# Attention scores and post-mixing on 64x128 tiles of the matmul array, v's products on 128x64 tiles, a group's query rows spaced out

## The chip, the core and the metric

The kernel runs on one core of a Trainium2 chip. The metric is the device time of one execution in microseconds (us). A core has a matmul engine (TensorE, PE in the rows; PEld is its weight load), VectorE (DVE), ScalarE (ACT), GpSimd (POOL) and SyncE (SP), and 16 DMA engines that the queues of SP, ACT and POOL share.

## What is computed

Attention whose heads are mixed before and after the softmax ("talking heads"), then a two-layer network with a PReLU. Batch 4, 12 heads, 448 positions, head width 64; all in float32, the network's weights in float64.

```python
scores = scale * np.matmul(q, k.transpose(0, 1, 3, 2))
scores = np.einsum('bhij,hg->bgij', scores, w_pre)
attn = softmax(scores)                       # over j
attn = np.einsum('bhij,hg->bgij', attn, w_post)
x = np.matmul(attn, v)                       # heads side by side: 1792 x 768
h = x @ w_in                                 # 768 x 2048
out = (np.maximum(h, 0) + alpha * np.minimum(h, 0)) @ w_out
```

## The kernel before

The first stage, up to some 523 us, is the attention; a second, from 555 us, is the network (lines 394 to 494), which the change does not touch. Between them lies the tail of the attention and the first loads of the network.

The attention works on chunks of query rows, four per batch (`CHUNKS`, line 27: 110, 110, 110 and 118 rows), 16 in all, and inside a chunk on groups of 10 rows, 180 in all, two of them per step, 90 steps. What happens to a group:

- `qk` (line 139): for a pair of heads, one in the upper 64 rows of the array and one in the lower, the chunk's scores for all 448 keys. A matmul here has at most 64 stationary columns, so a chunk's rows are cut in two (64 and 46, or 64 and 54), and the four pieces stand in the four 64x64 quarters of the array. `qk_out` (150) copies them from PSUM to the tile `st`, where a query row is a partition that holds all 12 heads. Six such pairs make a chunk.
- `relay` (159): a DMA from SBUF to SBUF takes the 10 rows of a group, partitions r to r+9 of `st` with 12 heads each, to 120 partitions of one of eight `sr` buffers. 180 relays of 210 KB are issued alternately by SP and POOL, three steps ahead of their use (`relays`, 338; a relay waits until the mix four steps back has read its buffer).
- `mix` (164): the mixing before the softmax, 64x64 tiles, two groups of a step side by side, four matmuls. `rmax`, `exp`, `norm` (173 to 194): row maximum on VectorE, two exponentials with their sums on ScalarE, and the scaling of the post-mixing weights `r`.
- `post` (196): two steps later the mixing after the softmax, with `e` as the stationary operand, 64 keys (columns) at a time, and 60 columns of `r` streamed: 28 matmuls per step. Its result is the one PSUM tile `pa`, keys in partitions; `post_out` (207) copies it into `at` with two ScalarE copies.
- `pv` (216): when a chunk is complete, for six heads at a time, v's product: 42 matmuls, in which `v` is the stationary operand (64 keys by 64 columns of one head) and `at` is streamed. Even and odd 64-key blocks are summed in two PSUM banks apart, and `pv_out` (230) copies one with ScalarE and adds the other with VectorE. The result goes to DRAM.

Each float32 matmul of the program is two weight loads and two matmul instructions in the trace. `qk` and `pv` use one PSUM tile in turns (`ps_s`, one buffer). The order is written by hand in `step` (349): the mix of the next step, the relays, VectorE's and ScalarE's part of the softmax, the first scores or v job of the step, `post` and `post_out`, further jobs. Beside this, VectorE rounds the network's weights from float64 (`round_f64`, seven instructions for each of 32 pieces), which POOL loads (`cr`) and SP stores (`wsc`).

Of the kernel before, what the change touches and what calls it, by code (L numbers as in the profile page):

```python
# [22 lines left out]
GI = 10  # L23
# [3 lines left out]
CHUNKS = [(0, 110), (110, 110), (220, 110), (330, 118)]  # L27
CW = 118
# [3 lines left out]
NS = 4  # L32
NJ = S // 64
# [27 lines left out]
def talking_heads_prelu(ctx: ExitStack, tc: tile.TileContext, q, k, v, w_pre, w_post, mask, w_in, w_out, alpha, out):  # L61
# [60 lines left out]
    def load_q(ci, dmas=None):  # L122
        b, c = chunk_list[ci]
        c0, cn = CHUNKS[c]
        q_t[ci] = qp.tile([128, NP, CW], F32, tag="q", name=f"q{ci}")
        for hf in range(2):
            dma = dmas[hf] if dmas else nc.gpsimd
            dma.dma_start(out=q_t[ci][64 * hf:64 * hf + 64, :, :cn],
                          in_=q[b, :, H * c0 + NP * hf * cn:H * c0 + NP * (hf + 1) * cn])

    def load_v(b):
        v_t[b] = vp.tile([128, NS, DM], F32, tag="v", name=f"v{b}")
        nf = S // 128
        nc.gpsimd.dma_start(out=v_t[b][:, :nf, :], in_=v[b, :nf * 128].rearrange("(s p) n -> p s n", p=128))
        nc.gpsimd.dma_start(out=v_t[b][:S - nf * 128, nf, :], in_=v[b, nf * 128:])
# [3 lines left out]
    def qk(ci, p, ps_pool=None):  # L139
        b, c = chunk_list[ci]  # L140
        cn = CHUNKS[c][1]
        ps = (ps_pool or ps_s).tile([128, 2, 512], F32, tag="m" if ps_pool else "s", name=f"s{ci}_{p}")
        for lo in range(0, cn, 64):
            hi = min(lo + 64, cn)
            for hf in range(2):
                r = slice(64 * hf, 64 * hf + 64)
                nc.tensor.matmul(ps[lo:hi, hf, :S], q_t[ci][r, p, lo:hi], k_t[b][r, p, :], start=True, stop=True)  # L147
        u_t["qk", ci, p] = ps
# [10 lines left out]
    def relay(n, dma):  # L159
        ci, r = groups[n]  # L160
        sr_t[n] = sr_b[n % NSR]
        dma.dma_start(out=sr_t[n][SR0:SR0 + GP], in_=s_t[ci][r:r + GI])  # L162
# [33 lines left out]
    def post(m):  # L196
        e, r = e_t.pop(m), r_t.pop(m)
        for u in range(2):
            for jb in range(NJ):
                s, c = divmod(jb, 2)  # L200
                for g in range(2):
                    h = slice(64 * g, 64 * g + 64)
                    dst = pa[64 * c:64 * c + 64, g, s * GP:(s + 1) * GP].rearrange("p (h i) -> p h i", h=H)
                    nc.tensor.matmul(dst[:, :, HI * u:HI * u + HI], e[h, u, 64 * jb:64 * jb + 64],  # L204
                                     r[h, u].rearrange("p (h i) -> p h i", h=H), start=True, stop=True)

    def post_out(m):
        for g in range(2):
            n = 2 * m + g
            ci, r = groups[n]  # L210
            if n == first[ci]:
                a_t[ci] = ap_.tile([128, NS, H, CW], F32, tag="a", name=f"at{ci}")
            dst = a_t[ci].rearrange("p s h i -> p (s h) i")[:, :, r:r + GI]
            nc.scalar.copy(dst, pa[:, g, :NS * GP].rearrange("p (s i) -> p s i", i=GI))  # L214

    def pv(ci, hx, ps_pool=None):
# [71 lines left out]
    with tc.manual_schedule():  # L288
# [23 lines left out]
        nc.vector.memset(pa, 0.0)  # L312
# [218 lines left out]
```

## Time and profile before

| | us |
|---|---|
| Three runs | 1031.63, 1038.42, 1039.06; median 1038.42 |
| Profiled execution, first to last instruction | 1038.9 |
| first stage, from the first mix to the last | 27 to 523: 496 |
| between the stages | 523 to 555: 32 |
| second stage | 555 to 1039: 484 |

The profiled execution's span lies 0.5 us above the median, and the parts are read as parts of that span. Over the whole span PE is busy 84%, PEld 66%, DVE 48%, ACT 43% and POOL 34%.

How to read the rows: "busy" is the time in which at least one instruction of the kind ran. "Idle <-X" is time in which an engine did nothing, and X what ended it; "issue" means that it waited for nothing that the profile shows. PEclk is the granted share of TensorE's full clock. The DMA share is the mean busy share of the 16 DMA engines. An x84 behind a form counts instructions, and sizes are partitions x elements; "64*64" is the piece of the array that a matmul uses, rows by columns.

### The profile page before, as it was taken

What the parts mean: (1) busy time and instruction counts of PE and PEld (TensorE: products, weight loads), DVE (VectorE), ACT (ScalarE), POOL (GpSimd) and SP (SyncE); (2) the same over time, 40 slices, a digit from 0 to 9 for tenths busy, and PEclk for the clock granted to TensorE, in tenths of its full rate; (3) what the DMA queues carried; (4) which work ended last, traced back from release to release, by engine and by line L of the source; (5) the groups of instructions that cost most, each with busy time, mean ns of one, the idle gap of its engine ahead of it and who ended that gap; (6) DMA issues with size and microseconds to landing.
All of it is one profiled execution on the core that took longest, in us unless ns stands there. A gap on an engine that the chain in (4) does not pass through costs nothing.

```text
span 1038.9 us, 26286 instructions
## 1 busy us (share of the span) xinstructions
PE 869.1 (84%) x11540; PEld 687.8 (66%) x11540; DVE 500.2 (48%) x886; ACT 441.6 (43%) x870; POOL 348.7 (34%) x305
## 2 busy tenths in 40 slices
PE   4656767867868687778666999999999999999998
PEld 2134444544535355455455999999999999999997
DVE  3454666656657376758624224632265224542222
ACT  1453666655657466648342232323233323232322
POOL 3121222222212122211004455554455454545452
PEclk9687898988889798889796999999999999999999
DMA  7698878897899977898618600020001000010001
GB/s 149 154 185 193 173 190 204 220 220 179 167 228 213 200 191 181 186 247 176 145 32 316 271 1 19 1 89 1 1 19 63 27 1 9 9 54 1 1 1 53
DMA packets 55209, 123.86 MB, mean 119 GB/s; under 512 B 21080, under 2 KB 38840, under 8 KB 54712
## 3 DMA queue, kind: packets, MB, share of 16 engines
q0 software_dynamic: 15232, 59.01, 25.7%
q1 hardware_dynamic: 38546, 60.12, 20.7%
q10 hardware_dynamic: 1318, 3.08, 1.2%
q8 instruction: 90, 1.47, 0.6%
q14 instruction: 23, 0.19, 0.1%
HBM read 59.85 MB, written 23.59 MB: 80 GB/s over the span
## 4 chain that ended last, share of the span: by engine, by line
PE 67%; DMA 16%; ACT 7%; issue 5%; DVE 4%; SPq 1%; POOL 0%; ACTq 0%; DVEq 0%; POOLq 0%
PE h L435 23%; PE acc L460 23%; DMA sr<-st 14%; PE s L147 7%; PE x L226 6%; PE m L170 4%; PE pa L204 4%; ACT st L155 3%; ACT at L214 2%; ACT e L182 1%; DMA xr<-x 1%; DMA wb<-in_w_post_dram 1%; DMA cr<-in_w_out_dram 1%; DVE xe L236 1%; DVE nm L175 1%
## 5 line engine op out<-in xcount | busy, mean ns | idle before, releaser
L435 PE MATMUL h<-xs,wi 128*128 128x448 f32 x1152 | 251.4, 371 | 12.6 <-DVE xs L425 11.3
L460 PE MATMUL acc<-g,wo 128*128 128x448 f32 x1152 | 248.2, 368 | 0.0
L435 PEld LDWEIGHTS h<-xs,wi 128*128 128x128 f32 x1152 | 218.4, 190 | 35.4 <-issue 11.5
L460 PEld LDWEIGHTS acc<-g,wo 128*128 128x128 f32 x1152 | 216.2, 188 | 21.8
L413 POOL TENSOR_TENSOR wi<-wr,wi 128x768 fp32r<-128x768 f32 x64 | 118.6, 1853 | 269.8 <-ACT wi L412 269.8
L204 PEld LDWEIGHTS pa<-r,e 64*64 64x64 f32 x5040 | 115.4, 146 | 79.6 <-issue 55.4
L175 DVE TENSOR_REDUCE nm<-m 128x2 f32<-128x896 f32 x90 | 97.9, 1088 | 135.7 <-PE m L170 135.5
L444 DVE TENSOR_SCALAR t<-h,alpha_sb 128x448 f32<-128x448 f32 x64 | 43.8, 684 | 245.7 <-PE h L435 245.7
L204 PE MATMUL pa<-r,e 64*64 64x60 f32 x5040 | 121.9, 234 | 43.6 <-issue 33.8
L170 PE MATMUL m<-sr,wk 64*64 64x448 f32 (+1 forms) x720 | 111.6, 650 | 50.4 <-DMA sr<-st 43.2
L446 ACT CAST g<-t 128x448 fp32r<-128x448 f32 x64 | 36.3, 567 | 275.2 <-DVE t L445 275.2
L162 POOL DMA_DIRECT2D sr<-st x88 | 54.2, 617 | 276.9 <-PE m L170 185.0
L147 PE MATMUL s<-k,q 64*46 64x448 f32 (+2 forms) x768 | 112.7, 640 | 39.5 <-ACT st L155 27.8
L214 ACT COPY at<-pa 128x480 f32<-128x480 f32 x180 | 93.2, 572 | 82.2 <-PE pa L204 82.0
L413 POOL TENSOR_TENSOR wo<-wr,wo 128x768 fp32r<-128x768 f32 x64 | 123.8, 1935 | 7.6 <-ACT wo L412 5.9
L182 ACT ACTIVATE e<-m,nm 128x448 f32<-128x448 f32 x180 | 113.7, 646 | 14.2 <-DVE nm L175 14.2
L226 PEld LDWEIGHTS x<-at,v 64*64 64x64 f32 x2688 | 88.2, 146 | 37.6 <-issue 20.3
L155 ACT COPY st<-s 110x896 f32<-110x896 f32 (+1 forms) x93 | 84.6, 909 | 63.0 <-PE s L147 55.6
L226 PE MATMUL x<-at,v 64*64 64x110 f32 (+1 forms) x2688 | 92.6, 280 | 18.5 <-issue 13.3
L147 PEld LDWEIGHTS s<-k,q 64*64 64x64 f32 (+2 forms) x768 | 27.5, 140 | 92.3 <-ACT st L155 70.9
L170 PEld LDWEIGHTS m<-sr,wk 64*64 64x64 f32 (+1 forms) x720 | 29.3, 151 | 77.5 <-issue 64.7
L412 ACT CAST wo<-wr 128x768 fp32r<-128x768 f32 x64 | 53.8, 841 | 62.3 <-PE acc L460 62.3
(46 smaller groups left out, 564.1 us busy)
## 6 DMA issues: line engine op xcount, KB each, us to landing
sr<-st SPq DMA_DIRECT2D x89, 210.0 KB
sr<-st POOLq DMA_DIRECT2D x88, 210.0 KB, 9.7
cr<-in_w_in_dram POOLq DMA_DIRECT2D x16, 768.0 KB, 11.5
cr<-in_w_out_dram POOLq DMA_DIRECT2D x16, 768.0 KB, 10.1
wsc<-ct SPq DMA_DIRECT2D x32, 384.0 KB
wr<-wsc SPq DMA_DIRECT2D x14, 768.0 KB
xr<-x SPq DMA_DIRECT2D x24, 224.0 KB
out_dram<-o SPq DMA_DIRECT2D x24, 224.0 KB
```

Of the source, the lines that this page charges most:

```text
L147: nc.tensor.matmul(ps[lo:hi, hf, :S], q_t[ci][r, p, lo:hi], k_t[b][r, p, :], start=True, stop=True)
L155: copy(dst[:cn, p], u_t.pop(("qk", ci, p))[:cn, :, :S])
L162: dma.dma_start(out=sr_t[n][SR0:SR0 + GP], in_=s_t[ci][r:r + GI])
L170: nc.tensor.matmul(ps[hf:hf + 64, u, :S], wk[r, :], g[r, :], start=True, stop=True)
L175: nc.vector.tensor_reduce(out=nm, in_=m_t[m][:, :, :S], axis=AX.X, op=ALU.max, negate=True)
L182: nc.scalar.activation(out=e_t[m][:, u], in_=m_t[m][:, u, :S], func=AF.Exp, bias=nm_t[m][:, u:u + 1], scale=1.0, accum_out=se_t[m][:, u:u ...
L204: nc.tensor.matmul(dst[:, :, HI * u:HI * u + HI], e[h, u, 64 * jb:64 * jb + 64], r[h, u].rearrange("p (h i) -> p h i", h=H), start=True, s ...
L214: nc.scalar.copy(dst, pa[:, g, :NS * GP].rearrange("p (s i) -> p s i", i=GI))
L226: nc.tensor.matmul(ps[64 * t:64 * t + 64, r, cl * CW:cl * CW + cn], v_t[b][pr, s, h * D:(h + 1) * D], a_t[ci][pr, s, h, :cn], start=(s == ...
L413: nc.gpsimd.tensor_tensor(t[:, 1], w, t[:, 0], ALU.subtract)
L435: nc.tensor.matmul(ps[:, :S], w[:, tw, cc * 128:(cc + 1) * 128], x[:, tx, cc, :], start=(i == 0), stop=(i == 3 * NCC - 1))
L460: nc.tensor.matmul(accs[c][:, :S], w[:, tw, c * 128:(c + 1) * 128], g[:, tg], start=(f == 0 and i == 0), stop=(f == NFC - 1 and i == 2))
```

## The change

A chunk has 120, 120, 120 and 90 rows (the last two ranges share two rows, which are computed twice). Its groups are no longer consecutive rows: with 12 groups, group r takes rows r, r+12, r+24 and so on, with 9 groups r, r+9 and so on. In `at` the rows of a group stand side by side, so a chunk's rows are in another order there, and `pv_out` puts them back as it copies. `qk` and `post` use the array as two halves of 64 rows by 128 columns, with up to 120 rows of queries and 112 keys per weight load; `pv` uses all rows (112 keys) and two column halves, in one PSUM bank, so that the addition on VectorE falls away; its six heads are copied out in three copies, by ScalarE for the first half of the heads and by VectorE for the second. `v` is loaded by one DMA onto 112 partitions.

```diff
-CHUNKS = [(0, 110), (110, 110), (220, 110), (330, 118)]
-CW = 118
+CHUNKS = [(0, 120), (120, 120), (240, 120), (358, 90)]
+CW = 120
+JW = S // NS
...
-        for r in range(0, cn, GI):
-            groups.append((ci, min(r, cn - GI)))
+        groups += [(ci, r) for r in range(CHUNKS[c][1] // GI)]
...
 def load_v(b):
-        nc.gpsimd.dma_start(out=v_t[b][:, :nf, :], in_=v[b, :nf * 128].rearrange("(s p) n -> p s n", p=128))
-        nc.gpsimd.dma_start(out=v_t[b][:S - nf * 128, nf, :], in_=v[b, nf * 128:])
+        nc.gpsimd.dma_start(out=v_t[b], in_=v[b].rearrange("(s p) n -> p s n", p=JW))
...
 def qk(ci, p, ps_pool=None):
-        for lo in range(0, cn, 64):
-            hi = min(lo + 64, cn)
-            for hf in range(2):
-                r = slice(64 * hf, 64 * hf + 64)
-                nc.tensor.matmul(ps[lo:hi, hf, :S], q_t[ci][r, p, lo:hi], k_t[b][r, p, :], start=True, stop=True)
+        for hf in range(2):
+            r = slice(64 * hf, 64 * hf + 64)
+            nc.tensor.matmul(ps[:cn, hf, :S], q_t[ci][r, p, :cn], k_t[b][r, p, :], start=True, stop=True)
...
 def relay(n, dma):
-        dma.dma_start(out=sr_t[n][SR0:SR0 + GP], in_=s_t[ci][r:r + GI])
+        dma.dma_start(out=sr_t[n][SR0:SR0 + GP], in_=s_t[ci][r:CHUNKS[chunk_list[ci][1]][1]:CHUNKS[chunk_list[ci][1]][1] // GI])
...
 def post(m):
-            for jb in range(NJ):
-                s, c = divmod(jb, 2)
+            for s in range(NS):
                 for g in range(2):
                     h = slice(64 * g, 64 * g + 64)
-                    dst = pa[64 * c:64 * c + 64, g, s * GP:(s + 1) * GP].rearrange("p (h i) -> p h i", h=H)
-                    nc.tensor.matmul(dst[:, :, HI * u:HI * u + HI], e[h, u, 64 * jb:64 * jb + 64],
+                    dst = pa[:JW, g, s * GP:(s + 1) * GP].rearrange("p (h i) -> p h i", h=H)
+                    nc.tensor.matmul(dst[:, :, HI * u:HI * u + HI], e[h, u, JW * s:JW * s + JW],
                                      r[h, u].rearrange("p (h i) -> p h i", h=H), start=True, stop=True)
...
 def pv(ci, hx, ps_pool=None):
-                    for r in range(2 if 2 * s + 1 < NJ else 1):
-                        pr = slice(64 * r, 64 * r + 64)
-                        nc.tensor.matmul(ps[64 * t:64 * t + 64, r, cl * CW:cl * CW + cn], v_t[b][pr, s, h * D:(h + 1) * D],
-                                         a_t[ci][pr, s, h, :cn], start=(s == 0), stop=(2 * s + 2 + r >= NJ))
+                    nc.tensor.matmul(ps[64 * t:64 * t + 64, 0, cl * CW:cl * CW + cn], v_t[b][:, s, h * D:(h + 1) * D],
+                                     a_t[ci][:, s, h, :cn], start=(s == 0), stop=(s == NS - 1))
...
 def pv_out(ci, hx):
-        src = u_t.pop(("pv", ci, hx))[:, :, :3 * CW].rearrange("p r (c i) -> p r c i", c=3)
-        nc.scalar.copy(xe[:, :, :cn], src[:, 0, :, :cn])
-        nc.vector.tensor_tensor(xe[:, :, :cn], src[:, 1, :, :cn], xe[:, :, :cn], ALU.add)
+        copy = nc.vector.tensor_copy if hx else nc.scalar.copy
+        for cl in range(3):
+            copy(xe[:, cl, :cn].rearrange("p (k g) -> p g k", k=GI),
+                 ps[:, 0, cl * CW:cl * CW + cn].rearrange("p (g k) -> p g k", k=GI))
```

On PE, before, around a v job (m is the mix's result, pa that of `post`, x that of `pv`, s the scores; an x28 counts matmuls of the program):

```order
L204 MATMUL pa<-r_580,e_523 64x12x5 x28
L170 MATMUL m_681<-sr_112,wk 64x448 x2
L170 MATMUL m_681<-sr_113,wk 64x448 x2
L226 MATMUL x_0_699<-at_360,v_276 64x110 x42
L204 MATMUL pa<-r_640,e_584 64x12x5 x28
L147 MATMUL s_0_775<-k_127,q_448 64x448 x2
L147 MATMUL s_0_775<-k_127,q_448 54x448 x2
```

On PE, now, at the same place:

```order
L198 MATMUL pa<-r_492,e_449 112x12x5 x16
L165 MATMUL m_570<-sr_112,wk 64x448 x2
L165 MATMUL m_570<-sr_113,wk 64x448 x2
L218 MATMUL x_0_588<-at_325,v_260 64x120 x24
L198 MATMUL pa<-r_538,e_496 112x12x5 x16
L165 MATMUL m_643<-sr_114,wk 64x448 x2
L165 MATMUL m_643<-sr_115,wk 64x448 x2
L142 MATMUL s_0_663<-k_127,q_432 90x448 x2
```

The mix keeps its four matmuls of 64x64; `post` goes from 28 to 16, `pv` from 42 to 24 and a pair of scores from 4 to 2, and pieces of three shapes now follow each other.

On ACT, before, around the copy of a v job (xe), and then now:

```order
L182 ACTIVATE e_1542,se_1543<-m_1476,nm_1488 128x448 x2
L235 COPY xe_0_1589<-x_0_1546 128x3x110
L214 COPY at_1523<-pa 128x48x10 x2
L155 COPY st_1627<-s_0_1622 110x2x448
L155 COPY st_1627<-s_1_1629 110x2x448
```

```order
L177 ACTIVATE e_1260,se_1261<-m_1193,nm_1205 128x448 x2
L229 COPY xe_0_1289<-x_0_1264 128x12x10 x3
L208 COPY at_1309<-pa 112x48x10 x2
L150 COPY st_1214<-s_2_1312 120x2x448
L177 ACTIVATE e_1336,se_1337<-m_1245,nm_1258 128x448 x2
```

One copy of 330 columns has become three of 120 in this half of the heads; in the other half ACT has none, and VectorE the three.

## Rows read from the trace of the kernel before

**Rows 1.** Busy time of each engine by stage (us; x instructions).

```profile
core 0: us, PE busy (x) PEld busy (x) DVE busy (x) ACT busy (x) POOL busy (x), PEclk, DMA share, GB/s
27.00:523.00 496.00, 363.68 (x8684) 233.57 (x8684) 303.77 (x603) 285.83 (x641) 96.54 (x157) 0.86 0.83 191
523.00:555.00 32.00, 14.90 (x485) 13.07 (x485) 6.24 (x15) 11.44 (x25) 4.69 (x3) 0.79 0.34 109
555.00:1039.00 484.00, 478.74 (x2304) 434.36 (x2303) 181.62 (x251) 140.31 (x201) 237.48 (x126) 0.99 0.12 44
```

**Rows 2.** The same view: a dense and a gappy stretch of the first stage.

```profile
100.00:118.00 18.00, 16.14 (x486) 11.28 (x479) 13.45 (x29) 13.31 (x30) 2.42 (x4) 0.97 0.78 167
217.00:238.00 21.00, 10.55 (x203) 7.28 (x199) 7.37 (x17) 7.71 (x19) 1.78 (x3) 0.75 0.89 200
```

**Rows 3.** What ended PE's idle time, 27 to 523: total us, times, longest.

```profile
PE m L170 <- DMA sr<-st: 43.2, 11, 9.7
PE pa L204 <- issue: 33.8, 14, 6.2
PE s L147 <- ACT st L155: 27.8, 34, 3.2
PE x L226 <- issue: 13.3, 6, 4.9
PE m L170 <- issue: 6.2, 2, 3.8
```

**Rows 4.** DMA queues, 40 to 540: packets, MB, share of 16 engines.

```profile
q0 software_dynamic: 14127, 55.77, 50.3%
q1 hardware_dynamic: 27462, 35.52, 29.2%
q8 instruction: 72, 1.18, 1.0%
```

**Rows 5.** Timeline of PE inside a v job, from 217 on.

```profile
221.49 0.89 PE L226 MATMUL x<-at,v 64*64 64x110 f32 x13 [3.70 <-issue]
```

**Rows 6.** DMA in 40 slices, 18 to 28 (first relays), then 548 to 560.

```profile
DMA  0002296996987798979965859774131567678365
GB/s 0 0 0 43 65 208 115 165 186 122 194 158 122 130 186 167 203 132 324 229 111 114 128 104 161 82 72 79 29 57 57 122 157 139 157 125 171 132 171 122
...
DMA  9869889999999999996420002000002859468988
GB/s 198 197 162 258 287 323 306 424 340 387 426 405 394 399 400 382 418 400 257 167 102 0 27 0 55 0 0 0 0 0 30 108 125 364 155 102 179 300 234 297
```

**Rows 7.** All relays (tile sr): us from issue to landing, POOL's.

```profile
DMA to landing us min/median/max: 5.3/9.7/21.7
```

**Rows 8.** Timeline of PE: start us, length us; a whole post, a v job.

```profile
203.86 1.14 PE L204 MATMUL pa<-r,e 64*64 64x60 f32 x56
...
206.14 2.38 PE L226 MATMUL x<-at,v 64*64 64x110 f32 x81
```

**Rows 9.** Weight loads of scores, post and network: ns min/median/max, forms sampled.

```profile
L147 PEld LDWEIGHTS s<-k,q x768: 114/129/228, 7.8 to 482.8; 64*64 64x64 f32 x101, 64*46 64x46 f32 x81, 64*54 64x54 f32 x10
L204 PEld LDWEIGHTS pa<-r,e x5040: 129/135/228, 46.3 to 533.8; 64*64 64x64 f32 x194
L435 PEld LDWEIGHTS h<-xs,wi x1152: 187/188/333, 554.3 to 1027.1; 128*128 128x128 f32 x192
```

**Rows 10.** Matmuls of post and of v's products, whole span (page): busy us, mean ns, idle.

```profile
L204 PE MATMUL pa<-r,e 64*64 64x60 f32 x5040 | 121.9, 234 | 43.6 <-issue 33.8
...
L226 PE MATMUL x<-at,v 64*64 64x110 f32 (+1 forms) x2688 | 92.6, 280 | 18.5 <-issue 13.3
```

**Rows 11.** Copies out of PSUM, 40 to 540: busy us, mean ns, idle before.

```profile
L214 ACT COPY at<-pa 128x480 f32<-128x480 f32 x180 | 93.2, 572 | 82.2 <-PE pa L204 82.0
...
L235 ACT COPY xe<-x 128x330 f32<-128x330 f32 x24 | 10.4, 435 | 53.0 <-PE x L226 53.0
L236 DVE TENSOR_TENSOR xe<-x,xe 128x330 f32<-128x330 f32 x24 | 12.0, 500 | 40.6 <-ACT xe L235 40.5
```

More of the change, by code (lines that the diff above doesn't have):

```diff
@@ L26 @@
 HP = HI * H
-CHUNKS = [(0, 110), (110, 110), (220, 110), (330, 118)]
-CW = 118
+CHUNKS = [(0, 120), (120, 120), (240, 120), (358, 90)]
+CW = 120
+QOFF = [H * sum(n for _, n in CHUNKS[:c]) for c in range(len(CHUNKS))]
 NCC = DM // 128
@@ L32 @@
 NS = 4
-NJ = S // 64
+JW = S // NS
 SR0 = 4
@@ L71, in talking_heads_prelu @@
         first.append(len(groups))
-        cn = CHUNKS[c][1]
-        for r in range(0, cn, GI):
-            groups.append((ci, min(r, cn - GI)))
+        groups += [(ci, r) for r in range(CHUNKS[c][1] // GI)]
     NG, NC = len(groups), len(chunk_list)
@@ L128, in load_q @@
             dma.dma_start(out=q_t[ci][64 * hf:64 * hf + 64, :, :cn],
-                          in_=q[b, :, H * c0 + NP * hf * cn:H * c0 + NP * (hf + 1) * cn])
+                          in_=q[b, :, QOFF[c] + NP * hf * cn:QOFF[c] + NP * (hf + 1) * cn])
     def load_v(b):
-        v_t[b] = vp.tile([128, NS, DM], F32, tag="v", name=f"v{b}")
-        nf = S // 128
-        nc.gpsimd.dma_start(out=v_t[b][:, :nf, :], in_=v[b, :nf * 128].rearrange("(s p) n -> p s n", p=128))
-        nc.gpsimd.dma_start(out=v_t[b][:S - nf * 128, nf, :], in_=v[b, nf * 128:])
+        v_t[b] = vp.tile([JW, NS, DM], F32, tag="v", name=f"v{b}")
+        nc.gpsimd.dma_start(out=v_t[b], in_=v[b].rearrange("(s p) n -> p s n", p=JW))
     u_t = {}
@@ L211, in post_out @@
             if n == first[ci]:
-                a_t[ci] = ap_.tile([128, NS, H, CW], F32, tag="a", name=f"at{ci}")
-            dst = a_t[ci].rearrange("p s h i -> p (s h) i")[:, :, r:r + GI]
-            nc.scalar.copy(dst, pa[:, g, :NS * GP].rearrange("p (s i) -> p s i", i=GI))
+                a_t[ci] = ap_.tile([JW, NS, H, CW], F32, tag="a", name=f"at{ci}")
+            dst = a_t[ci].rearrange("p s h i -> p (s h) i")[:, :, GI * r:GI * r + GI]
+            nc.scalar.copy(dst, pa[:JW, g, :NS * GP].rearrange("p (s i) -> p s i", i=GI))
     def pv(ci, hx, ps_pool=None):
@@ L233, in pv_out @@
         xe = xep.tile([128, 3, CW], F32, tag="xe", name=f"xe{ci}_{hx}")
-        src = u_t.pop(("pv", ci, hx))[:, :, :3 * CW].rearrange("p r (c i) -> p r c i", c=3)
-        nc.scalar.copy(xe[:, :, :cn], src[:, 0, :, :cn])
-        nc.vector.tensor_tensor(xe[:, :, :cn], src[:, 1, :, :cn], xe[:, :, :cn], ALU.add)
+        ps = u_t.pop(("pv", ci, hx))
+        copy = nc.vector.tensor_copy if hx else nc.scalar.copy
+        for cl in range(3):
+            copy(xe[:, cl, :cn].rearrange("p (k g) -> p g k", k=GI),
+                 ps[:, 0, cl * CW:cl * CW + cn].rearrange("p (g k) -> p g k", k=GI))
         later.append(lambda: nc.sync.dma_start(
@@ L311, in talking_heads_prelu @@
             nc.vector.memset(t[:SR0], 0.0)
-        nc.vector.memset(pa, 0.0)
         for i, w in enumerate((w_pre, w_post)):
```

## The prediction

> **What bounds the kernel now.** I read the busy times by stage first. The second stage is one stream of matmuls (478.7 of 484 us busy, clock 0.99) and holds nothing that the change touches [rows 1]. So the question is the 496 us of the first stage. [...] A stretch without gaps has PE busy 16.1 of 18 us at clock 0.97; one with gaps 10.6 of 21 us at 0.75 [rows 2]. Next come the waits, for what makes the gaps: PE waits 43.2 us for relays, 53.3 us (33.8 + 13.3 + 6.2) for "issue", and 27.8 us for ScalarE's copies of the scores [rows 3]. The issue waits fall in the middle of a run of equal matmuls, where no data is missing: 3.70 us inside one v job [rows 5]. I take them for missing instructions: a queue named "instruction" moves 72 packets of 16.4 KB [rows 4] while about 18,800 instructions run (8684 + 8684 + 603 + 641 + 157 [rows 1]), some 260 per packet, over nine tenths of them PE's. Such a packet has to pass the same DMA engines as the relays. So 96.5 us of PE's gaps come from a crowded DMA, and PE's own work is the next bound right behind.
>
> **The change part by part**, against the profiled span of 1038.9 us; the median, 1038.42, is the same to 0.05%.
>
> Relays. The bytes and the issues stay, the source partitions change from ten neighbours to ten spread over 90 to 120. When relays are nearly alone, the queues are busy at 6 to 9 tenths and move about 130 to 200 GB/s; the network's first loads, at 9 tenths, move about 400 [rows 6]. So a relay keeps engines busy at half the rate that they can do. That its ten neighbouring source rows are the cause is not shown by these rows. [...] Bounds by rows: unchanged (landing 9.7 us, waits of 43.2 us) or at the full rate, with landings near the smallest seen, 5.3 us [rows 7], far less than the three steps of lead (3 x 496/90 = 16.5 us); the waits would then go. I take 10 of 43 us left.
>
> Instructions. Program matmuls: post 90 x 28 to 90 x 16, v 32 x 42 to 32 x 24, scores 96 x 4 to 96 x 2, mix 360 as before: 4608 to 2760, and as many loads, so 40% fewer PE instructions and some 45 packets for 72. A post now uses its 112 instructions in 1.14 us [rows 8], so a packet of 260 lasts 2.6 us there, less than the wait of 3.7; with 64 instructions in 1.75 us (below) it lasts 7 us. Bounds: the waits fall with the packets (53 to 33), or to none; I take 10, since a longer stock and a less crowded DMA work together. Both kinds of wait: 96.5 to 20, **-76 us**.
>
> Post. This term goes the other way. A load of 46 columns takes 114 ns, one of 64 takes 129, one of 128 takes 187 [rows 9]: 0.83 to 0.91 ns per column. A post's fullest quarter of the array has 16 load-matmul pairs; from first to last, 1.14 us [rows 8] less the 0.23 us of a single matmul [rows 10], is 15 x 61 ns, and 64 columns at 0.83 are 53 of these. So the load is the pace already, and not the 60 columns streamed. In a half of 128 columns there are again 16 pairs, now with 112 columns to load: 93 + 8 = 101 ns each, 15 x 101 + 0.23 = 1.75 us, 0.61 more; 90 times **+55 us**. The lower bound is 0, if a half loads its two column blocks at once as two quarters do. I stay with the row. Part of it is covered: `post` stands ahead of scores that wait for ScalarE's copy, 27.8 us [rows 3]; I count 20 of these as absorbed, **-20 us**. Without that cover they are lost.
>
> Scores: 448 columns streamed as before, the first load 56 columns wider, 47 ns by the same slope, 96 times: **+4.5 us**. V's products: 24 pairs per column half as per quarter before; 81 matmuls in 2.38 us [rows 8], less the 0.28 us of one [rows 10], some 22 steps, 95 ns per step of 110 columns. That is far over a load of 64 columns, so columns count, and those sum to 450 rows for 448 per batch: 0.
>
> Shapes. Mix on quarters, scores and post on column-wide halves, v on row-wide halves: two switches per step and one more per v job, 2 x 90 + 32 = 212. No row shows a switch without another wait beside it. Below, a switch costs nothing; above, the last matmul has to leave (0.23 us, of which some 0.05 its columns) and a first load follows in the open (0.13 [rows 9]): 0.31 us, 66 us in all. I take 0.1, **+20 us**, as many switches fall where PE waits anyway. [...]
>
> Copies of v's products: by 572 ns for 480 columns and 435 for 330 [rows 11] a ScalarE copy of 120 is 244 ns, three 0.73 us, in place of 0.435 + 0.50 on two engines in turn. The shared PSUM tile is free no later, ScalarE gains in one half what it loses in the other: 0. If the scattered writes cost double, 16 x 0.73 us, 12 us, lie on an ACT that has 210 us idle.
>
> Clock: with the gaps cut, from 0.86 towards the dense stretch's 0.97; at 0.93, 364 x (1 - 0.86/0.93) = 27 us, of which two thirds, since loads and the ends of matmuls don't all scale: **-18 us**. The tail has four posts in the open behind the last mix: **+3 us**.
>
> Sum: -76 + 55 - 20 + 4.5 + 20 - 18 + 3 = -31.5, 1038.9 to 1007.
>
> **The rivals.** (a) The gaps vanish altogether and the wider loads are hidden. For it: ACT and DVE, under 310 us each, don't forbid it, and a dense stretch runs 486 matmuls in 18 us against 8684 in 496. Against: PE would be the bound, with 364 + 55 us. All waits and half of post's net 35 us gone and no price for switches: -96 + 17 + 4.5 - 18 + 3 = -90, 949 us. (b) The relays don't gain from the spacing: 33 us of relay waits come back, and nothing else changes: 1040. For it: the low rate could come from reading and writing SBUF at once, as these first relays do, whatever the rows. (c) Slower: every switch drains, 0.31 us in place of 0.1, at 212 places on PE between mix, post and v, +45 us: 1052. For it: the first matmul of every post or mix now overlaps the stage ahead of it, which drained shapes couldn't. Against: where PE waits for ScalarE, a drained array costs nothing. [...] It decides from 0.25 us per switch on (31.5/212 + 0.1), and is slower by 1% from 0.30.
>
> **How the numbers follow.** The forecast, with its own range of 982 to 1028, has 0.45; (a) 0.18; (b) 0.18; (c) 0.19. About 1% is what a measurement of this kernel can tell from no change. Faster by over 1% holds (a) and nearly all of the forecast, with a little of (b) where fewer instructions alone do it: 0.62. Within 1%: most of (b) and edges of the forecast, 0.20. Slower: most of (c), 0.18. The range reaches close to (a) and past (c): 956 to 1056.
>
> **What would show it.** Right: a post of 32 matmul instructions lasts about 1.75 us; some 45 instruction packets; issue and relay waits of PE near 20 us in all; landings of relays well under 9.7 us; the clock of the first stage above 0.9; first mix to last mix about 470 us. Wrong: a post near 1.1 us (load term gone, rival a); landings as before (b); matmuls at a change of shape that start 0.3 us later than the end of a load would let them, at most places (c).

## The result, and the profile of the changed kernel

The changed kernel takes 984.70 us in the median (978.04 to 987.82, four runs), against 1038.37 (1031.63 to 1039.06) before: a ratio of 0.9557, 95% interval 0.9455 to 0.9658. The forecast was 1007, with a range of 956 to 1056. In the table are all kernels that ran; those of one block ran on one chip, beside runs of the kernel before on that chip, and an empty cell stands for the median above it. The medians are over all executions, while the ratios leave out those in which the chip ran in its slower state.

| kernel | median us | before there | ratio, 95% interval |
|---|---|---|---|
| changed kernel | 984.70 | 1038.37 | 0.9557 [0.9455, 0.9658] |
| e1_spacing | 1002.28 | 1047.36 | 0.9613 [0.9535, 0.9691] |
| e2_tiles | 1024.12 | | 0.9782 [0.9662, 0.9902] |
| e3_post_quarters | 958.69 | | 0.9189 [0.9099, 0.9279] |
| e4_spacing2 | 990.08 | | 0.9493 [0.9402, 0.9584] |
| e5_spacing_clean | 999.23 | 1039.83 | 0.9624 [0.9562, 0.9686] |
| e6_quarters_pvrows | 970.22 | | 0.9332 [0.9271, 0.9393] |
| e7_k_parts | 955.96 | | 0.9214 [0.9146, 0.9283] |
| changed_again | 979.27 | | 0.9437 [0.9360, 0.9514] |
| e8_spacing_q_order | 979.27 | 1034.64 | 0.9455 [0.9407, 0.9503] |
| e9_changed_q_order | 987.80 | | 0.9469 [0.9358, 0.9579] |
| e10_post_quarters_q_order | 958.87 | | 0.9259 [0.9162, 0.9356] |
| e11_q_order_k_parts | 950.97 | | 0.9185 [0.9129, 0.9242] |

The profiled execution of the changed kernel has a span of 985.9 us, 1.2 above the median. Its busy times by stage, with the columns of [rows 1]:

```profile
24.00:475.00 451.00, 398.16 (x5172) 263.03 (x5176) 299.99 (x619) 281.48 (x655) 93.11 (x153) 0.92 0.74 209
475.00:511.00 36.00, 22.77 (x329) 20.78 (x321) 4.84 (x15) 11.19 (x27) 4.11 (x3) 0.74 0.29 99
511.00:986.00 475.00, 469.50 (x2304) 433.88 (x2304) 182.40 (x251) 140.02 (x201) 237.10 (x126) 0.99 0.12 45
```

Against [rows 1], of the 53 us between the spans 45 are the first stage (496 to 451), 3 come before it, the stretch between gives 4 back, and 9 are the second stage (484 to 475), which the change does not touch; the last section comes back to these. Inside the first stage PE is busy 34.5 us longer (398.2 for 363.7) with 40% fewer instructions, and idle 79.5 us less (52.8 for 132.3): the change trades gaps for work. What ended PE's idle time in that stage (total us, times, longest):

```profile
PE m L165 <- DMA sr<-st: 29.9, 7, 10.7
PE s L142 <- ACT st L150: 23.0, 27, 8.5
```

Beside [rows 3], the three "issue" lines (53.3 us) are gone altogether, the relays' 43.2 us have become 29.9, and the scores' wait for ScalarE is nearly what it was. Each relay line holds one wait that lies ahead of the stage, that of the first mix, 9.7 us before and 5.9 now (timelines of PE, before and then now):

```profile
27.60 3.25 PE L170 MATMUL m<-sr,wk 64*64 64x448 f32 x12 [9.68 <-DMA sr<-st]
```

```profile
23.88 3.25 PE L165 MATMUL m<-sr,wk 64*64 64x448 f32 x12 [5.92 <-DMA sr<-st]
```

After the first mix PE waits 33.5 us for relays before and 24.0 now. The DMA queues, 40 to 480 (packets, MB, share of 16 engines):

```profile
q0 software_dynamic: 13554, 54.68, 46.3%
...
q8 instruction: 42, 0.69, 0.7%
```

and the relays from issue to landing:

```profile
DMA to landing us min/median/max: 2.4/5.8/17.1
```

Nearly as many bytes as in [rows 4] take less of the engines' time (q0: 46.3% of 440 us are 204 us, 50.3% of 500 were 252), a relay lands after 5.8 us for 9.7 [rows 7], and 42 instruction packets do what took 72. Last, a dense piece of PE's timeline (start us, length us):

```profile
103.15 2.68 PE L218 MATMUL x<-at,v 112*64 112x120 f32 x48 [0.23 <-ACT at L208]
105.76 1.78 PE L198 MATMUL pa<-r,e 64*112 64x60 f32 x32
107.48 0.98 PE L165 MATMUL m<-sr,wk 64*64 64x448 f32 x8
108.39 1.02 PE L142 MATMUL s<-k,q 64*120 64x448 f32 x4
109.24 1.69 PE L198 MATMUL pa<-r,e 64*112 64x60 f32 x32
110.77 0.97 PE L142 MATMUL s<-k,q 64*120 64x448 f32 x4
```

A post lasts 1.69 us (1.14 in [rows 8]): 15 steps of (1.69 - 0.26)/15 = 95 ns for 112 columns to load (0.26 us is one of its matmuls), while its matmul streams 60 columns as before. The timeline also prices a change of shape. Where the shape stays (108.39 + 1.02 against 109.24; 109.24 + 1.69 against 110.77), the next piece starts 0.17 and 0.16 us before the last one ends. Where it changes (post to mix at 107.48, mix to scores at 108.39), 0.06 and 0.07 us before. So a change costs 0.10 us here. It is the same all through the stage: without a wait between them, pieces of equal shape overlap by 0.17 to 0.25 us in the median in the kernel before, pieces of unequal shape by 0.07 now.

### The profile page after: what moved, and what is told of

Same layout as the page of the kernel before. It is cut to its first block, busy times and chain, and to the rows that moved or that the text cites. A ratio compares the mean times of both kernels' runs of the same rounds, so it can differ in the third digit from the quotient of the medians.

```text
span 985.9 us, 18954 instructions
## 1 busy us (share of the span) xinstructions
PE 905.0 (92%) x7844; PEld 725.9 (74%) x7844; DVE 495.0 (50%) x901; ACT 436.7 (44%) x886; POOL 343.8 (35%) x301
## 3 DMA queue, kind: packets, MB, share of 16 engines
q8 instruction: 62, 1.02, 0.4%
## 5 line engine op out<-in xcount | busy, mean ns | idle before, releaser
L453 PEld LDWEIGHTS acc<-g,wo 128*128 128x128 f32 x1152 | 216.4, 188 | 17.1
L198 PEld LDWEIGHTS pa<-r,e 64*112 64x112 f32 x2880 | 157.6, 179 | 40.0 <-issue 19.6
L198 PE MATMUL pa<-r,e 64*112 64x60 f32 x2880 | 161.2, 263 | 5.1 <-ACT at L208 5.1
L437 DVE TENSOR_SCALAR t<-h,alpha_sb 128x448 f32<-128x448 f32 x64 | 43.8, 684 | 236.0 <-PE h L428 236.0
L208 ACT COPY at<-pa 112x480 f32<-112x480 f32 x180 | 92.8, 569 | 99.1 <-PE pa L198 99.1
L142 PE MATMUL s<-k,q 64*120 64x448 f32 (+1 forms) x384 | 105.2, 619 | 25.8 <-ACT st L150 23.0
L165 PE MATMUL m<-sr,wk 64*64 64x448 f32 x720 | 97.8, 607 | 29.9 <-DMA sr<-st 29.9
L150 ACT COPY st<-s 120x896 f32<-120x896 f32 (+1 forms) x93 | 85.0, 914 | 63.0 <-PE s L142 55.7
L218 PEld LDWEIGHTS x<-at,v 112*64 112x64 f32 x1536 | 82.1, 148 | 27.5 <-ACT at L208 12.0
L218 PE MATMUL x<-at,v 112*64 112x120 f32 (+1 forms) x1536 | 89.2, 278 | 4.3 <-ACT at L208 1.8
L142 PEld LDWEIGHTS s<-k,q 64*120 64x120 f32 (+1 forms) x384 | 29.8, 186 | 79.4 <-ACT st L150 53.5
L165 PEld LDWEIGHTS m<-sr,wk 64*64 64x64 f32 x720 | 20.4, 139 | 60.3 <-issue 42.4
```

What stands on the lines that cost most here:

```text
L142: nc.tensor.matmul(ps[:cn, hf, :S], q_t[ci][r, p, :cn], k_t[b][r, p, :], start=True, stop=True)
L150: copy(dst[:cn, p], u_t.pop(("qk", ci, p))[:cn, :, :S])
L165: nc.tensor.matmul(ps[hf:hf + 64, u, :S], wk[r, :], g[r, :], start=True, stop=True)
L198: nc.tensor.matmul(dst[:, :, HI * u:HI * u + HI], e[h, u, JW * s:JW * s + JW], r[h, u].rearrange("p (h i) -> p h i", h=H), start=True, sto ...
L208: nc.scalar.copy(dst, pa[:JW, g, :NS * GP].rearrange("p (s i) -> p s i", i=GI))
L218: nc.tensor.matmul(ps[64 * t:64 * t + 64, 0, cl * CW:cl * CW + cn], v_t[b][:, s, h * D:(h + 1) * D], a_t[ci][:, s, h, :cn], start=(s == 0) ...
```

## The experiments

Theory: relays read from spread rows hold the DMA engines for less time, which ends waits; fewer instructions end the issue waits; wider loads make PE's own work longer. Rival 1: the spacing does nothing, and the tiles do it all. Rival 2: the tiles cost more than they bring. First the two halves of the change apart.

**e1_spacing**: the kernel before with the new chunks and the spaced relays; tiles stay 64x64, and `post_out` puts the rows back.

```diff
-CHUNKS = [(0, 110), (110, 110), (220, 110), (330, 118)]
+CHUNKS = [(0, 120), (120, 120), (240, 120), (358, 90)]
...
-        for r in range(0, cn, GI):
-            groups.append((ci, min(r, cn - GI)))
+        groups += [(ci, r) for r in range(CHUNKS[c][1] // GI)]
...
-        dma.dma_start(out=sr_t[n][SR0:SR0 + GP], in_=s_t[ci][r:r + GI])
+        dma.dma_start(out=sr_t[n][SR0:SR0 + GP], in_=s_t[ci][r:CHUNKS[chunk_list[ci][1]][1]:CHUNKS[chunk_list[ci][1]][1] // GI])
...
-            dst = a_t[ci].rearrange("p s h i -> p (s h) i")[:, :, r:r + GI]
+            dst = a_t[ci].rearrange("p s h i -> p (s h) i")[:, :, r:CHUNKS[chunk_list[ci][1]][1]:CHUNKS[chunk_list[ci][1]][1] // GI]
```

> The relays' spaced rows alone: the kernel before with the new chunks and the spaced groups, and every matmul still on 64x64 quarters (the copy after post writes with the spacing, so that the rows of at stand in order). Theory: part of the gain is the relays', part the fewer instructions', and the tiles have a price (post's wider loads, changes of shape). So landings of POOL's relays fall from 9.7 to about 6 us, PE's waits for relays from 43 to about 25 us, its waits for instructions from 53 to about 30 us, post stays at 1.14 us, and the time is about 990 us. Rival A, the spacing does nothing and all comes from the instructions: landings 9.7 us, 1038 us. Rival B, the instructions do nothing and all comes from the relays: under 950 us, since the tiles' price is not paid.

Measured: 0.9613 [0.9535, 0.9691], with its new chunks; relays land after 6.1 us, PE waits 17.6 us for them and 26.3 us for issue. So the spacing works without the tiles, and rivals A and B are out. Both waits fell further than expected and the gain is no larger, for the scattered copies of `post_out` had become long (1050 ns for 572), which the changed kernel's are not (569 in the mean), and PE waits 27.8 us for them (6.8 before):

```profile
L213 ACT COPY at<-pa 128x480 f32<-128x480 f32 x180 | 169.6, 1050 | 33.0 <-PE pa L203 31.5
```

**e2_tiles**: the changed kernel with neighbouring rows.

```diff
-        dma.dma_start(out=sr_t[n][SR0:SR0 + GP], in_=s_t[ci][r:CHUNKS[chunk_list[ci][1]][1]:CHUNKS[chunk_list[ci][1]][1] // GI])
+        dma.dma_start(out=sr_t[n][SR0:SR0 + GP], in_=s_t[ci][GI * r:GI * r + GI])
...
-            copy(xe[:, cl, :cn].rearrange("p (k g) -> p g k", k=GI),
-                 ps[:, 0, cl * CW:cl * CW + cn].rearrange("p (g k) -> p g k", k=GI))
+            copy(xe[:, cl, :cn], ps[:, 0, cl * CW:cl * CW + cn])
```

> The tiles alone: the changed kernel with groups of ten neighbouring rows (the copies of v's products then don't reorder). Theory: 45 packets of instructions, no more waits inside runs of equal matmuls, but landings near 9.7 us, waits for relays of 40 us or more, post at 1.7 us: about 1025 us. Rival A: about 985 us, as the changed kernel. Rival B: above 1060 us, the price of the tiles without any gain.

Measured: 0.9782 [0.9662, 0.9902], a gain of 1 to 3%. Landings, and waits of PE and ScalarE, 24 to 505:

```profile
DMA to landing us min/median/max: 5.2/9.3/21.9
```

```profile
PE s L142 <- ACT st L150: 36.8, 28, 8.4
PE m L165 <- DMA sr<-st: 25.1, 7, 10.0
...
PE pa L198 <- issue: 1.5, 3, 0.8
```

```profile
ACT st L150 <- DMA sr<-st: 21.8, 5, 8.5
```

The landings are those of before, so the rows and not the tiles shorten them. The issue waits are gone (53.3 to 1.5) though the DMA is no less crowded than it was (q0 takes 55.8% from 40 to 480, by the same view as above): fewer instructions do that by themselves. One expectation fails: after the first mix PE waits only 25.1 us for relays, not 40 or more, and hardly more than the changed kernel's 24.0. The long landings show on ScalarE: it waits 21.8 us until relays have read `st` (5.9 before, 7.3 in the changed kernel), and PE's wait for its copies of the scores is 36.8 us for 23.0. So with these tiles most of what the spacing takes from PE's waits comes by way of ScalarE.

**e4_spacing2**: the changed kernel with a group's rows spaced by 2 (20 partitions in place of 90 to 120).

```diff
+    def rows_of(n):
+        ci, r = groups[n]
+        if r == 8 and CHUNKS[chunk_list[ci][1]][1] == 90:
+            return slice(80, 90)
+        lo = 2 * GI * (r // 2) + r % 2
+        return slice(lo, lo + 2 * GI - 1, 2)
...
+        dma.dma_start(out=sr_t[n][SR0:SR0 + GP], in_=s_t[ci][rows_of(n)])
```

> The changed kernel with a group's ten rows spaced by 2 (r, r+2 to r+18; in the last chunk one group of neighbours), the copy after post puts them in order. [...] So landings lie between the two, about 7 us, and the time between the tiles alone and the changed kernel, about 1000 us. Rival: what counts is only that rows are not neighbours (a conflict of adjacent partitions): landings 5.8 us and 985 us, as with 12.

Measured: 0.9493 [0.9402, 0.9584], not to be told from the changed kernel by its time; the landings stand between:

```profile
DMA to landing us min/median/max: 3.5/7.6/20.6
```

9.3 us for rows side by side, 7.6 spaced by 2, 5.8 spaced by 12 or 9, with the same tiles: the cost goes with how far the source rows spread. What in the chip makes it so is not shown, and the 7 us that were expected are the author's estimate. The shortest landings say it best, 5.2, 3.5 and 2.4 us: in every kernel with rows spaced by 12 or 9 the shortest is 2.4 or 2.5, while the median differs from kernel to kernel, from 5.8 to 7.5 us.

**e3_post_quarters**: the changed kernel with `post` as before on 64x64 tiles (and so v's products on 128 rows).

```diff
...
-            for s in range(NS):
+            for jb in range(NJ):
+                s, c = divmod(jb, 2)
...
-                    dst = pa[:JW, g, s * GP:(s + 1) * GP].rearrange("p (h i) -> p h i", h=H)
-                    nc.tensor.matmul(dst[:, :, HI * u:HI * u + HI], e[h, u, JW * s:JW * s + JW],
+                    dst = pa[64 * c:64 * c + 64, g, s * GP:(s + 1) * GP].rearrange("p (h i) -> p h i", h=H)
+                    nc.tensor.matmul(dst[:, :, HI * u:HI * u + HI], e[h, u, 64 * jb:64 * jb + 64],
```

> The changed kernel with post alone back on 64x64 quarters (28 matmuls, 64 keys per load), v's products still on all rows (128 keys, the last block 64). Theory: the load of 112 columns paces post, so post goes from 1.69 back to 1.14 us, PE gets 50 us less work in the first stage; with 2160 more loads and as many more matmul instructions, some 60 packets of instructions for 45 and a few waits for them. Net about 965 us. Rival: post's load is covered by ScalarE's work, and the time stays within 1% of 985 us; or the instructions weigh more than the load, and it is slower than 995 us.

Measured: 0.9189 [0.9099, 0.9279], below the changed kernel's interval. The wide loads of `post` are a cost, and 61 instruction packets instead of 42 (40 to 480) brought back only 12.0 us of issue waits (24 to 452). The run also pays for its v products: a job on 128 rows, with a last block of 64, takes 3.32 us for 2.68 in the changed kernel.

**e5_spacing_clean** and **e6_quarters_pvrows**. e5 is e1 with the rows put back in `pv_out`, per head pair a ScalarE copy and a VectorE addition from two banks; e6 puts v's products on 128 rows and into one bank, so that the addition goes, keeps scores and `post` on 64x64, and copies as the changed kernel does. From e5's edit of the kernel before, and then from e6's of the changed kernel (beside that of e3):

```diff
...
-        nc.scalar.copy(xe[:, :, :cn], src[:, 0, :, :cn])
-        nc.vector.tensor_tensor(xe[:, :, :cn], src[:, 1, :, :cn], xe[:, :, :cn], ALU.add)
...
+        for cl in range(3):
+            dst = xe[:, cl, :cn].rearrange("p (k g) -> p g k", k=GI)
+            nc.scalar.copy(dst, ps[:, 0, cl * CW:cl * CW + cn].rearrange("p (g k) -> p g k", k=GI))
+            nc.vector.tensor_tensor(dst, ps[:, 1, cl * CW:cl * CW + cn].rearrange("p (g k) -> p g k", k=GI), dst, ALU.add)
```

```diff
...
-            nc.tensor.matmul(ps[:cn, hf, :S], q_t[ci][r, p, :cn], k_t[b][r, p, :], start=True, stop=True)
...
+                nc.tensor.matmul(ps[lo:hi, hf, :S], q_t[ci][r, p, lo:hi], k_t[b][r, p, :], start=True, stop=True)
```

> The spacing alone once more, without the slow copy: e1_spacing's copies after post wrote with the spacing and took 1050 ns for 572. Here every matmul stands on 64x64 quarters as before, a group's rows are side by side in at, and the order is put right as v's products are copied out (three ScalarE copies and three additions on VectorE per six heads). Theory: ScalarE gets 75 us less work than in e1_spacing and PE no longer waits 25 us for the copy after post; waits for instructions stay near 22 us and for relays near 18 us: a ratio to before of about 0.93, better than the changed kernel's 0.956. Rival: the copies were covered, and the ratio stays at 0.96; then the tiles carry a gain of their own.

> e3_post_quarters with the scores on 64x64 quarters too: only v's products keep a new tile (all rows, 128 keys). Theory of the shapes: from mix to scores and from scores to mix the start now follows 465 ns after the last matmul's start where equal shapes give 373, some 92 ns per change; without these changes about 140 of them go, 13 us, and the loads of the scores are 47 ns shorter, 4 us; 384 more matmul and load instructions cost little. Ratio to before about 0.905, against 0.919. Rival: the changes are covered by ScalarE's work, ratio as e3_post_quarters, 0.92 or above.

Measured: 0.9624 [0.9562, 0.9686] and 0.9332 [0.9271, 0.9393]. Both miss. e5 has its rival's number; its copies and additions (some 355 ns each in the mean) hold the one PSUM tile that scores and v's products share, and PE waits for them, 24.1 us in 16 waits for the additions, which e6 has not. That the tiles carry a gain of their own, as the rival would have it, does not follow, and e8 decides it. e6 is not below e3 but above it, in its rival's range; the last section shows one reason, a piece of 26 columns.

**changed_again**: the changed kernel unaltered, on the chip of e5 to e7.

> The changed kernel itself, unaltered, on the chip of these runs: ratio to before about 0.956 as measured, so that the others can be set against it.

Measured: 0.9437 [0.9360, 0.9514]; its first stage ends some 11 us earlier than in the profile above, and its relay waits are 26.4 us (29.9 above). So 10 us between single profiles of two kernels say little, and the ratios are what counts.

**e8_spacing_q_order**: the spacing alone, with nothing to put back. q's rows stand in another order in DRAM, so that spaced partitions of `st` hold consecutive rows; the tiles and copies are those of before, the chunks and relays those of e1.

```diff
...
-            dst = a_t[ci].rearrange("p s h i -> p (s h) i")[:, :, r:r + GI]
+            dst = a_t[ci].rearrange("p s h i -> p (s h) i")[:, :, GI * r:GI * r + GI]
...
-        "q": _np.concatenate([qt[:, :, :, a:a + n].reshape(B, D, H * n) for a, n in CHUNKS], axis=2),
+        "q": _np.concatenate([qt[:, :, :, [a + GI * (p % (n // GI)) + p // (n // GI) for p in range(n)]].reshape(B, D, H * n) for a, n in CHUNKS], axis=2),
```

> The kernel before with its own tiles, the new chunks and spaced relays; q's rows stand in another order in DRAM, so that spaced partitions of st hold consecutive rows and no copy puts anything back. Theory (in e1_spacing and e5_spacing_clean the copies that reorder gave a part of the gain back): ratio about 0.945 (0.93 to 0.955), landing of the relays near 6 us, PE's waits for relays near 20 us. Rival (the reorder was cheap, and what the tiles of the changed kernel add is the rest): ratio as in those two runs, 0.960 to 0.965.

Measured: 0.9455 [0.9407, 0.9503], as the theory had it: the reorder had cost e1 and e5 some 1.6%. Relays land after 7.0 us, not near 6. The ratio is also the changed kernel's own (0.9557 and 0.9437, e9 0.9469): once the rows are spread, the tiles add nothing to the time that these runs can show. Why, its first stage and PE's waits there show (views and columns as above):

```profile
24.00:474.00 450.00, 354.32 (x8620) 210.62 (x8616) 303.20 (x605) 287.17 (x643) 95.93 (x157) 0.95 0.74 210
```

```profile
PE s L146 <- ACT st L154: 25.1, 31, 7.6
PE pa L203 <- issue: 18.4, 11, 4.0
PE m L169 <- DMA sr<-st: 18.2, 5, 6.0
PE x L225 <- issue: 14.8, 8, 5.4
...
PE s L146 <- issue: 3.6, 2, 1.9
PE m L169 <- issue: 3.0, 3, 1.3
```

450 us as against 451. Going on to the changed kernel's tiles takes away 39.8 us of issue waits (18.4 + 14.8 + 3.6 + 3.0) and adds 43.8 us of PE work (354.3 to 398.2). The relays' part, 43.2 to 18.2 us (33.5 to 12.3 after the first mix), is the spacing's. e8 carries some 21 us of PE work that neither kernel has (last section); without them, by estimate, the tiles would add some 65 us of work and cost more than they bring. No run shows that.

**e9_changed_q_order** and **e10_post_quarters_q_order**: the changed kernel with that order of q and one plain copy of 360 columns for six heads; and the same with `post` on 64x64.

```diff
...
-        for cl in range(3):
-            copy(xe[:, cl, :cn].rearrange("p (k g) -> p g k", k=GI),
-                 ps[:, 0, cl * CW:cl * CW + cn].rearrange("p (g k) -> p g k", k=GI))
+        copy(xe[:, :, :cn], ps[:, 0, :3 * CW].rearrange("p (c i) -> p c i", c=3)[:, :, :cn])
```

> The changed kernel, with q's rows in that order in DRAM and v's products copied in one plain copy of 360 columns per six heads, in place of three scattered ones of 120. If the reorder costs about what its copies last longer (3 x 405 = 1.2 us against some 0.47, 32 times, 24 us at most, a part of it hidden): ratio about 0.935 (0.925 to 0.945). Rival (the copies lie beside other work, as the prediction had it): ratio as the changed kernel, 0.944 to 0.956, within 0.5%.

> The same with post back on 64x64 tiles (v's products on 128 rows), so e3_post_quarters without the reorder. Theory (the load of 112 columns paces post, whatever else): ratio 0.905 to 0.915, about 2.5 to 3.5% under e9_changed_q_order. Rival (what post's quarters gain comes from somewhere that the plain copies gain too): no more than 1% under e9_changed_q_order, 0.92 to 0.93.

Measured: 0.9469 [0.9358, 0.9579] and 0.9259 [0.9162, 0.9356]. e9's ratio lies in its rival's range: in the changed kernel the scattered copies cost nothing that can be measured. Its interval reaches into the theory's range, so a cost of up to about 1% is not excluded. ACT and DVE, busy at most 300 of 451 us, have room for the copies; that this is the reason is not shown. e10 is 0.9259/0.9469 = 0.978 of e9, 22 us. The step is a little below the one expected, and the ratio itself lies in the rival's range. With e3 it shows that the wide loads of `post` cost more than the issue waits they save; its size is known to about 1%, for the two intervals all but touch. And e10's v products are busy 105.0 us where the changed kernel's are 89.2, so `post` alone gains more than the step shows. In e10's timeline a post takes 1.14 us again.

**e7_k_parts** and **e11_q_order_k_parts**: e6 and e10 with k loaded in six parts of two DMAs each.

```diff
...
+        for hf in range(2):
+            nc.gpsimd.dma_start(out=k_t[b][64 * hf:64 * hf + 64, i:i + 1, :],
+                                in_=k[b, :, (NP * hf + i) * S:(NP * hf + i + 1) * S])
...
-                at(first[ci] // 2 - 15, "load", load_k, b)
+                for i in range(6):
+                    at(first[ci] // 2 - 18 + 2 * i, "load", load_k_part, b, i)
```

> e6_quarters_pvrows with the next batch's k loaded in six parts of 2 x 112 KB over eleven steps, from three steps earlier on, in place of 2 x 672 KB in one step. Theory: the longest waits for relays that are left (6 to 11 us each) stand where k, v and the network's weights are loaded together, so with smaller parts the waits for relays fall from 20 to about 10 us: a ratio 0.01 below e6_quarters_pvrows. Rival: the bytes are the same and the waits only move: no change.

> e10_post_quarters_q_order with k loaded in six parts. Theory (the relay waits that are left stand where the two 0.69 MB loads of k fill the DMA engines, as e7_k_parts showed with 1.2%): longest landing of the relays near 12 us, waits for relays some 5 us less, ratio about 0.9 (0.89 to 0.905), the shortest of all. Rival (those waits move on to another load): within 0.5% of e10_post_quarters_q_order.

Measured: 0.9214 [0.9146, 0.9283] after e6's 0.9332, and 0.9185 [0.9129, 0.9242] after e10's 0.9259. The reason for trying was in the changed kernel's trace, around two of its loads of k (PE and POOL, then ACT and PE before another):

```profile
288.22 0.55 POOL L118 DMA_DIRECT2D k<-in_k_dram  x1
...
298.12 1.77 PE L165 MATMUL m<-sr,wk 64*64 64x448 f32 x8 [10.67 <-DMA sr<-st]
...
309.65 1.77 PE L165 MATMUL m<-sr,wk 64*64 64x448 f32 x8 [6.56 <-DMA sr<-st]
```

```profile
179.67 1.25 POOL L118 DMA_DIRECT2D k<-in_k_dram  x2
...
195.62 0.90 ACT L150 COPY st<-s 90x896 f32<-90x896 f32 x1 [7.25 <-DMA sr<-st]
...
196.57 1.80 PE L142 MATMUL s<-k,q 64*90 64x448 f32 x4 [8.50 <-ACT st L150]
```

17.2 of the 29.9 us of relay waits follow one load of k (its two DMAs are issued at 288 and 290 us), and the longest wait "for ScalarE" is a relay wait too: ACT could not write `st` before a relay had read it. With k in parts the longest landing is 12.4 us in e7 (19.5 in e6) and 13.4 in e11 (15.8), and the scores' longest wait is 1.3 us in e7 (8.4 in e6). After the first mix the relay waits fall from 15.4 to 8.7 us in e7, about as the theory had it, and the scores' line falls by as much, from 28.1 to 20.2. So e7's gain is shown (its slowest run, 958.1, is under e6's fastest, 966.0), and half of it came by way of ScalarE, which the theory did not name. In e11 the relay waits after the first mix fall from 24.4 to 10.7 us, more than expected, and its network starts 9.7 us earlier than e10's (467.4 for 477.1). But the ratio misses the 0.89 to 0.905 that was expected, its step of 0.8% lies between theory and rival, and its interval overlaps with e10's, so by its time the gain is not shown. e11 has the shortest median of all; e3, e7, e10 and e11 all lie below the changed kernel and the kernel before.

## Why the prediction was right, and where its terms were off

By the prediction's own sum (profile against profile, us):

| part | forecast | measured |
|---|---|---|
| PE's waits for relays and for issue in the first stage | -76 | -63.4 (87.4 to 24.0) |
| scores' wait for ScalarE, absorbed by `post` | -20 | -4.8 (27.8 to 23.0) |
| PE's work: post +55, scores +4.5, shapes +20, clock -18 | +61.5 | +34.5 |
| other idle time of PE in the first stage | 0 | -11.3 (17.1 to 5.8) |
| between the stages | +3 | +4 |
| before the stage 3, second stage 9 | 0 | -12 |
| sum | -31.5 | -53.0 |

The 96.5 us that the prediction puts into the first stage hold 9.1 that lie ahead of it, the wait of the first mix, and so do 5.9 of the 29.9 now. The mechanism was right: shorter relays and fewer instructions end waits, wider loads and changes of shape cost work, and the first is more than the second. That the sum came as near as it did is in part luck: the first two rows and the stretch between the stages missed by 29 us one way, the other rows by 50 us the other way.

- **Waits.** That spread rows would make the relays shorter was the author's estimate, which no row showed; with the same tiles a relay lands after 9.3 us from neighbouring rows (e2) and after 5.8 from spread ones. Direction and sum of the waits held, the parts less so: issue waits fell to 0 (10 taken), relay waits only to 29.9, or 24.0 after the first mix (10 taken). "Far less than the three steps of lead" is true of the median landing, 5.8 us, but the waits come from long landings (the longest takes 17.1 us), 17.2 us of them behind one load of k. A median says nothing of the waits that a tail makes.
- **Post.** The load paces it, as the prediction chose between its bounds: 1.75 us forecast, 1.69 measured, and with `post` back on quarters the kernel is 2 to 4% faster (e10 against e9, e3 against both measurements of the changed kernel). A load of 112 columns takes 169 ns at the least, one of 64 takes 129 [rows 9]. Over the stage `post` is busy 35.4 us longer (rows below), its part of the clock's gain included. The -20 us for cover by ScalarE's copies failed: only 4.8 us of those waits went, partly because the longest of them is no wait for ScalarE's work.
- **Shapes.** 0.10 us per change was taken and 0.10 is read. Rival (c) with 0.31 is out. The overlap shrinks by 0.10 us, from 0.17 to 0.07, a third of the 0.31 that the prediction had as its upper bound for a drained array, an estimate that no run shows.
- **V's products.** In a dense stretch a v job takes 2.61 us from its start to the next piece's (103.15 to 105.76), against at most 2.38 before [rows 8]: not 0 but at least 0.23 us. Over the stage it does not show, where v's matmuls are busy 8.1 us less than before.
- **PE's work and the clock.** The granted clock of the stage is 0.92, and 0.93 was taken. PE's matmuls by piece in the first stage, before and then now (busy us, mean ns, idle before):

```profile
L204 PE MATMUL pa<-r,e 64*64 64x60 f32 x4816 | 117.2, 235 | 40.2 <-issue 33.8 <-ACT at L214 6.1
L170 PE MATMUL m<-sr,wk 64*64 64x448 f32 (+1 forms) x712 | 110.6, 651 | 50.3 <-DMA sr<-st 43.2 <-issue 6.2
L147 PE MATMUL s<-k,q 64*46 64x448 f32 (+2 forms) x720 | 107.4, 646 | 34.7 <-ACT st L155 27.8 <-DVE r L192 3.4 <-DVE xe L236 2.5
L226 PE MATMUL x<-at,v 64*64 64x110 f32 (+1 forms) x2436 | 83.6, 279 | 16.1 <-issue 13.3 <-ACT st L155 1.8 <-ACT at L214 0.7
```

```profile
L198 PE MATMUL pa<-r,e 64*112 64x60 f32 x2752 | 152.6, 261 | 2.8 <-ACT at L208 2.8
L165 PE MATMUL m<-sr,wk 64*64 64x448 f32 x716 | 97.4, 608 | 29.9 <-DMA sr<-st 29.9
L142 PE MATMUL s<-k,q 64*120 64x448 f32 (+1 forms) x360 | 96.5, 615 | 23.7 <-ACT st L150 23.0
L218 PE MATMUL x<-at,v 112*64 112x120 f32 (+1 forms) x1344 | 75.5, 271 | 2.4 <-ACT st L150 1.5 <-ACT at L208 0.7
```

  `post` takes 35.4 us more, the other three 32.2 less, the mix among them 13.2 with the very same instructions. So the four together stay nearly the same (418.8 to 422.0). But before they overlapped by 55.1 us (418.8 - 363.7), and now by 23.8: the 34.5 us that PE is busy longer are nearly all lost overlap, 31.3 us, which the prediction had as its price for changes of shape, 20. What it had as +55 for `post`, +4.5 for the scores and -18 for the clock came out as 3.2 together. How much of that is the clock, 0.86 to 0.92, and how much fewer short stops inside a piece, is not shown. That this time does not all go with the clock, as the -18 has it, the trace of before shows for `post`: at a clock of 0.50 (68.4 to 69.9) its matmuls take 313 ns in the mean and its loads 214, at 1.00 (203.86 to 204.9) 223 and 134, so 1.4 and 1.6 times and not 2.
- **Copies.** Nothing, as forecast, though one of 120 columns takes 405 ns on ACT in the first stage and not 244; e9 finds no cost in it, to about 1%.
- **Rivals.** (a) fails on the work: PE is busy 398 us and the stage takes 451, with gaps of 53 us left. (b) is refuted by e1 and e8, and on the landings by e4. Nine of the 22 us between forecast and median lie in the second stage, which the change does not touch; the first stage was missed by 10.5 us (-45 measured, -34.5 forecast).

What the prediction did not see is that the change has a better half: the spacing alone gives 0.9455, and of the tiles the issue waits' gain and the cost of loads and changes of shape cancel.

## What to carry to other kernels

Price a new tile shape by its weight loads as well as by its instructions: here 40% fewer instructions ended 40 us of waits, and wider loads and changes of shape gave 44 back. The kernels that went below the changed one have narrow tiles for `post`, which streams 60 columns. Whether wide ones help the scores, which stream 448, is not shown: e7, without them, is within the intervals of e10 and e11. Count overlap as well: pieces of one shape ran into each other by 0.2 us, pieces of two shapes by 0.07. When a DMA reads a few SBUF rows, spread them over the partitions (ten rows landed after 5.8 us for 9.3 here), and choose the order in DRAM so that nothing has to be put back (0.9455 in e8, 0.9613 and 0.9624 with a reorder). Before counting on short transfers, look at what large load stands next to the longest landing, and cut that load (the longest landing went from 19.5 us in e6 to 12.4 in e7).

## What the runs showed that had not been expected

**A quarter with 26 columns doubles the scores.** In e1 and e5 to e8 a chunk of 90 rows is cut into 64 and 26 on 64x64 tiles. Its scores take 1.84 us at a time at which the mixes beside them take 0.98 (a piece of 120 rows, cut into 64 and 56, takes 0.97). In e8 (timeline of PE):

```profile
79.50 1.84 PE L146 MATMUL s<-k,q 64*64 64x448 f32 x8
81.27 0.98 PE L169 MATMUL m<-sr,wk 64*64 64x448 f32 x8
...
104.06 0.97 PE L146 MATMUL s<-k,q 64*64 64x448 f32 x8
```

Single matmuls last no longer, as its groups by shape show:

```profile
L146 PE MATMUL s<-k,q 64*64 64x448 f32 x360 | 93.5, 589 | 33.3 <-ACT st L154 25.1 <-DVE xe L235 3.7 <-issue 3.6
...
L146 PE MATMUL s<-k,q 64*26 64x448 f32 x96 | 23.9, 575 | 0.0
```

So it looks as if the pieces of 26 columns ran after those of 64 and not beside them, where those of 56 columns do; with 46 columns a pair took 0.99 us in the kernel before, at a clock of 1.00 (its timeline at 71.01). 24 pairs of 0.86 us (1.84 - 0.98) are 21 us, an estimate. It suggests that the spacing alone, with chunks cut otherwise, would be better than e8, and that part of what e10 gains on e6 is this. Such a cut was not tried.

**The second stage has two paces.** Untouched by every edit, at a granted clock of 1.00, it runs 292 matmuls in 60 us in the kernel before and 298 in the changed one, 2% apart; here the two kernels' windows in turn:

```profile
674.00:734.00 60.00, 60.00 (x292) 54.50 (x291) 18.86 (x28) 18.61 (x28) 30.30 (x17) 1.00 0.11 39
```

```profile
630.00:690.00 60.00, 60.00 (x298) 55.61 (x297) 17.17 (x27) 18.42 (x27) 30.61 (x17) 1.00 0.12 39
```

In the profiles the stage took about 475 us for the changed kernel (twice), e1, e4 to e8 and e10, and about 485 for before, e2, e3, e9 and e11; e1 and e2 ran on one chip, and so did e8 and e11. What sets the pace stays open; it is about 1% of the whole, so a difference of 1% between two kernels says nothing here, and e3 gains on the changed kernel in spite of it.

**Spreading the rows also shortens the issue waits.** With the instructions of before, the issue waits are 39.8 us in e8 and 26.3 in e1 (24 to 489) against 53.3: the DMA share of the stage falls from 0.83 to 0.74 in e8, as the prediction supposed, but that alone does not end them.
